# Loading the first q half as fp32 on ScalarE's queue and reordering the prologue copies of a linear-attention and SwiGLU kernel

## Chip, cores and metric

The kernel runs on one core of one Trainium2 chip. The metric is device time in microseconds of one execution. The median of eight runs before the change is 307.91 us (307.26 to 308.52).

## The reference

Linear attention with the feature map phi(x) = elu(x) + 1 feeds a SwiGLU feed-forward block.

```python
# q, k, v: (8, 8, 576, 64)
phi = lambda x: np.where(x > 0, x, np.exp(x) - 1.0) + 1.0
q_p, k_p = phi(q), phi(k)
kv  = np.einsum('bhsd,bhse->bhde', k_p, v)
z   = np.sum(k_p, axis=2)
num = np.einsum('bhsd,bhde->bhse', q_p, kv)
den = np.einsum('bhsd,bhd->bhs', q_p, z)[..., None] + 1e-06
x   = (num / den).transpose(0, 2, 1, 3).reshape(4608, 512)
g   = x @ w_gate                       # (512, 1536)
out = (g / (1 + np.exp(-g)) * (x @ w_val)) @ w_out   # (4608, 512)
```

## The kernel before

The 4608 tokens are handled in nine groups of 512. For each group the kernel needs x transposed (`xT`, four tiles of 128 features), runs the gate and value matmuls over twelve blocks of 128 hidden features (`l1`, with `l1_mm` for one matmul, line 291), and then the output matmuls (`l2`, line 450, and later a form with sums of blocks, line 506). The order on every engine is written out by hand: each call in the body appends its instructions to the queues of its engines, in the order of the calls, and nothing is rescheduled.

The attention of batch b is prepared while an earlier group is in the feed-forward block. Only batch 0 has nothing to hide behind. Its prologue is the part around the change. phi(x) is built as max(x, 0) + min(exp(x), 1). ScalarE makes the exp (`exp0`, line 598). VectorE makes the two terms (`term`, line 601: `k_max`, `k_min`, `q_max`, `q_min`). For the first half of the heads (`lp` = 0) the two k terms are added (`k_sum`, line 613); otherwise the two terms stay apart, `kp[1]`/`qp[1]` the max and `kp[0]`/`qp[0]` the min, and TensorE adds them in PSUM. The two halves of the heads are loaded apart:

- k's first half goes as fp32 from SyncE's queue into `k32`, a view of the space of `ws`, which is not needed until later;
- q's two halves, k's second half and v's halves go through GpSimd's queue (`load_0`, line 98) into fp16 tiles, followed by the weights `wg` and `wv` (`ld_w1`, line 111), later batches (line 95) and `wo` (`ld_w2`, line 115).

TensorE starts with `warm` (line 594), matmuls of constants into a bank that nobody reads. Then come `z0` (line 632), the sums of k's terms over the tokens, copied to `zz` by `z0_copy` (line 638); `t0_all` and `t0` (line 644), the transposes of q's terms against an identity, in banks `pV[0]`, `pV[1]` for the first half of the heads and `pG[0]`, `pG[1]` for the second, with the ninth block of columns in `pV[2]` and `pX[0]`; `t0_copy` (lines 651 and 653) moves them to `qT` by ScalarE or VectorE. `mm1` (line 174) makes k times v, copied to `R` by `r0_copies` (line 657). `den0` (line 264) makes the denominators, and ScalarE their reciprocals as exp of minus ln (lines 661 and 664). `num0` (line 264) makes the numerators, and `x00` (line 667) multiplies the two into `xT`. The second numerators (`num0(1)`) and the last 64 tokens' denominators stand behind the first step (i = 0) of the first four blocks' gate and value matmuls; the steps i = 1, 2 and 3 then follow.

Of the kernel before, what the change touches and what calls it, by code (L numbers as in the profile page):

```python
# [7 lines left out]
FP32 = mybir.dt.float32  # L8
FP16 = mybir.dt.float16
AF = mybir.ActivationFunctionType  # L10
ALU = mybir.AluOpType
AX = mybir.AxisListType

P = 128
# [3 lines left out]
def kernel(  # L18
# [10 lines left out]
    nc = tc.nc  # L29

    B, H, S, D = q.shape
# [4 lines left out]
    J = S // C  # L36
# [10 lines left out]
    def two(shape, dt, name, n=2):  # L47
        return [sb.tile(shape, dt, name=f"{name}_{i}") for i in range(n)]
# [3 lines left out]
    q16 = two([P, HL, J * D], FP16, "q16")  # L52
    v16 = two([P, HL, J * D], FP16, "v16")
    ek = sb.tile([P, HL, J * D], FP16, name="ek")
    eq = sb.tile([P, HL, J * D], FP16, name="eq")
    kp = two([P, J, HL * D], FP16, "kp")
    qp = two([P, J, HL * D], FP16, "qp")
# [18 lines left out]
    ws = sb.tile([P, 4, FB // 2, DM // 2], FP16, name="ws")  # L76
# [10 lines left out]
    pG = [pp.tile([P, 512], FP32, name=f"pG_{i}") for i in range(2)]  # L87
    pV = [pp.tile([P, 512], FP32, name=f"pV_{i}") for i in range(3)]
    pX = [pp.tile([P, 512], FP32, name=f"pX_{i}") for i in range(3)]

    def heads(src, b):
        return src[b].rearrange("(l a) (c j) d -> (a c) l (j d)", a=2, j=J)
# [4 lines left out]
    def load_0(src, dst, lp):  # L97
        nc.gpsimd.dma_start(out=dst[0][:, 2 * lp:2 * lp + 2, :], in_=heads(src, 0)[:, 2 * lp:2 * lp + 2, :])
# [63 lines left out]
    def terms_k(b, lp):  # L162

        return (kp[1], kp[0]) if (b, lp) == (0, 1) else (kp[b % 2],)

    def mm1(b, lp):
        if lp == 0:
            kvb[b] = ((pV[2], pX[0]), (pX[1], pV[2]), (pX[0], pX[1]), (pV[0], pG[0]), (pX[2], pV[2]))[min(b, 4)]
        for j in range(J):
            for (t, term_) in enumerate(terms_k(b, lp)):  # L170
                for hh in range(2):
                    rows = slice(C * hh, C * hh + C)
                    if b == 0:
                        nc.tensor.matmul(
                            out=kvb[b][hh][:, 256 * lp:256 * lp + P], lhsT=term_[rows, j, P * lp:P * lp + P],
                            rhs=v16[b][rows, 2 * lp:2 * lp + 2, D * j:D * j + D],
                            start=(j == 0 and t == 0), stop=(j == J - 1 and t == len(terms_k(b, lp)) - 1))
                        continue
                    for e in range(2):
                        w = D if b < 2 else D + 1  # L180
                        nc.tensor.matmul(  # L181
                            out=kvb[b][hh][D * e:D * e + D, 256 * lp:256 * lp + w],
                            lhsT=term_[rows, j, P * lp + D * e:P * lp + D * e + D],
                            rhs=v16[b][rows, 2 * lp + e, D * j:D * j + D] if b < 2 else vm[b % 2][rows, j, 2 * lp + e, :],
                            start=(j == 0), stop=(j == J - 1))
# [14 lines left out]
    def kv(b):  # L200
        c1 = D if b == 0 else 0
        return lambda i, e: R[b % 2][D * e:D * e + D, i, c1 * e:c1 * e + D]
# [55 lines left out]
    def corners(ps, lhs, b, j0, j1, lps=(0, 1)):  # L258

        for lp in lps:  # L260
            for hh in range(2):
                for e in range(2):
                    rows = slice(D * e, D * e + D)
                    nc.tensor.matmul(out=ps[2 * lp + e][C * hh:C * hh + C, :], lhsT=lhs(2 * lp + hh, e),  # L264
                                     rhs=qT[b % 2][rows, j0:j1, lp, C * hh:C * hh + C], start=True, stop=True)
# [301 lines left out]
                (p[3][1], c22[1], d22), (p[4][1], c12[1], d12), (lambda: fin_last(g),)]  # L567


    k32 = ws[:, :, :, :].rearrange("p m f c -> p (m f c)").bitcast(FP32)[:, 0:2 * J * D].rearrange("p (l x) -> p l x", l=2)  # L570
    nc.sync.dma_start(out=k32, in_=heads(k, 0)[:, 0:2, :])
    load_0(q, q16, 0)
    nc.gpsimd.iota(out=idx[:, :], pattern=[[-1, P]], base=0, channel_multiplier=1)
    load_0(q, q16, 1)
    load_0(k, k16, 1)
# [14 lines left out]
    A, V = "A", "V"  # L590

    def warm(n, dst):
        for _ in range(n):
            nc.tensor.matmul(out=dst[:, 0:256], lhsT=ones[:, :], rhs=sil[0][:, 0:256], start=True, stop=True)


    def exp0(src, e, lp):
        nc.scalar.activation(out=e[:, 2 * lp:2 * lp + 2, :], in_=src[:, 2 * lp:2 * lp + 2, :], func=AF.Exp, bias=0.0, scale=1.0)

    def term(src, dst, lp, val, op):  # L600
        nc.vector.tensor_scalar(
            out=dst[:, :, P * lp:P * lp + P].rearrange("p j (s d) -> p s j d", d=D),
            in0=src[:, 2 * lp:2 * lp + 2, :].rearrange("p s (j d) -> p s j d", d=D), scalar1=val, scalar2=None, op0=op)

    def k_max(lp):
        term(k16[0] if lp else k32, kp[1], lp, 0.0, ALU.max)

    def k_min(lp):
        term(ek, kp[0], lp, 1.0, ALU.min)
# [3 lines left out]
        nc.vector.tensor_tensor(out=kp[0][:, :, c], in0=kp[0][:, :, c], in1=kp[1][:, :, c], op=ALU.add)  # L613

    def q_max(b, lp):
        term(q16[b], qp[1], lp, 0.0, ALU.max)

    def q_min(lp):
        term(eq, qp[0], lp, 1.0, ALU.min)

    def zb0(b, lp, hh):
        if b == 0:
            return (pG if lp else (pV[2], pX[0]))[hh][:, P:P + D]
        return (pX[2], pV[2])[hh][:, D * lp:D * lp + D]

    def z0(b, lp):
        ts = terms_k(b, lp)
        for j in range(J):
            for t in ts:
                for hh in range(2):  # L630
                    rows = slice(C * hh, C * hh + C)
                    nc.tensor.matmul(out=zb0(b, lp, hh), lhsT=t[rows, j, P * lp:P * lp + P],
                                     rhs=ones[rows, 0:D], start=(j == 0 and t is ts[0]),
                                     stop=(j == J - 1 and t is ts[-1]))

    def z0_copy(b, lp):
        for hh in range(2):
            nc.vector.tensor_scalar(out=zz[:, 2 * lp + hh, :], in0=zb0(b, lp, hh), scalar1=1.0 / SC,
                                    scalar2=None, op0=ALU.mult)
# [7 lines left out]
    def t0_copy(src, lp, j0, j1, eng):  # L647
        dst = qT[0][:, j0:j1, lp, :]
        s3 = src[:, 0:P * (j1 - j0)].rearrange("p (j t) -> p j t", t=P)
        if eng == "A":  # L650
            nc.scalar.activation(out=dst, in_=s3, func=AF.Copy, bias=0.0, scale=1.0)
        else:
            nc.vector.tensor_copy(out=dst, in_=s3)

    def r0_copies(lp):
        for hh in range(2):
            nc.vector.tensor_copy(out=R[0][:, 2 * lp + hh, 0:P], in_=kvb[0][hh][:, 256 * lp:256 * lp + P])

    def ln0(src, dst):
        for i in range(len(src)):  # L660
            nc.scalar.activation(out=dst[:, i, :], in_=src[i], func=AF.Ln, bias=epst[:, 0:1], scale=1.0)

    def exp_neg(dst):
        nc.scalar.activation(out=dst, in_=dst, func=AF.Exp, bias=0.0, scale=-1.0)

    def x0(src, r, dst):
        nc.vector.scalar_tensor_tensor(out=dst, in0=src, scalar=1.0 / SC, in1=r, op0=ALU.mult, op1=ALU.mult)  # L667
# [3 lines left out]
    def den0(lp):  # L671
        corners({2 * lp + e: dbank0[e][:, :] for e in range(2)}, zs, 0, 0, 8, (lp,))
        ln0([b[:, :] for b in dbank0], rr[:, 2 * lp:2 * lp + 2, :])
        exp_neg(rr[:, 2 * lp:2 * lp + 2, :])

    def num0(lp):
        corners({2 * lp + e: nbank0[lp][e][:, :] for e in range(2)}, kv(0), 0, 0, 8, (lp,))

    def x00(lp, e):
        x0(nbank0[lp][e][:, :], rr[:, 2 * lp + e, :], xT[2 * lp + e][0][:, :])  # L680

    def t0_all(lp, t):
        for i in range(2):
            t0((pV, pG)[lp][i], lp, 4 * i, 4 * i + 4, (t,))
# [1 line left out]
    bank8 = (pV[2], pX[0])  # L686
    part8 = [slice(C * (i // 2), C * (i // 2) + C) for i in range(4)]

    warm(37, pX[1])
    exp0(k32, ek, 0)  # L690
    exp0(q16[0], eq, 0)
    exp0(q16[0], eq, 1)
    k_max(0)
    k_min(0)
    k_sum(0)
    q_max(0, 0)
    z0(0, 0)
    z0_copy(0, 0)
    q_max(0, 1)
    q_min(0)  # L700
    t0_all(0, 0)
    t0_all(0, 1)
    t0_copy(pV[0], 0, 0, 4, V)
    t0_copy(pV[1], 0, 4, 8, A)
    exp0(k16[0], ek, 1)
    t0_all(1, 0)
    warm(4, pX[1])
    q_min(1)
    k_max(1)
    t0_all(1, 1)  # L710
    for lp in range(2):
        t0(bank8[lp][:, 3 * P:4 * P], lp, 8, 9)
    t0_copy(pG[0], 1, 0, 4, V)
    t0_copy(pG[1], 1, 4, 8, A)
    den0(0)
    k_min(1)
    mm1(0, 0)
    r0_copies(0)
    for lp in range(2):
        t0_copy(bank8[lp][:, 3 * P:4 * P], lp, 8, 9, V)  # L720
    z0(0, 1)
    z0_copy(0, 1)
    num0(0)
    den0(1)
    mm1(0, 1)
    x00(0, 0)
    r0_copies(1)
    x00(0, 1)
    for c in (256, 512, 768, 1024):
        ld_w1(c, c + 256)  # L730
    ld_k(1)
# [280 lines left out]
```

## Time and profile before

| | before |
|---|---|
| median of 8 runs | 307.91 us |
| profiled execution | 308.52 us |
| its span, first to last instruction | 306.7 us |
| TensorE matmul busy | 297.2 us (97%) |
| VectorE busy | 250.9 us (82%) |
| ScalarE busy | 214.3 us (70%) |
| GpSimd busy | 49.8 us (16%) |
| TensorE idle in the first 20 us, mainly | 7.8 to 8.6 and 9.2 to 10.4 us |

Times in the profile are microseconds from the start of the span of one profiled execution. PE is TensorE, PEld its weight loads, DVE VectorE, ACT ScalarE, POOL GpSimd and SP SyncE. A row of the timeline gives start, duration, engine, line, operation and tiles, and in brackets the idle time before it with what ended it. `x18` means that 18 instructions are merged. A row of a stretch gives its length and then, for PE, PEld, DVE, ACT and POOL in this order, busy time and number of instructions, followed by the granted clock, the busy share of the DMA engines and the GB/s that they wrote. Where a stretch is asked for one line alone, only that line's engine is listed.

### The profile page before, as it was taken

Reading aid. Unit: us, or ns where it says so; the run is one execution under the profiler, and the core shown is the slowest. Engines: PE = TensorE matmul, PEld = TensorE weight load, DVE = VectorE, ACT = ScalarE, POOL = GpSimd, SP = SyncE. Lnnn points to the kernel's source line nnn. Section 1 sums busy time; section 2 is a strip of 40 time slices with the busy share of each in tenths; the row PEclk is TensorE's granted clock in tenths of the full one; section 3 lists DMA queues with packets and bytes.
Section 4 is the critical chain, followed back from the end, with each engine's and each line's share of the span. In section 5 each row is a group of like instructions: output and inputs, shape, how many; then the busy total and the mean of one; then the engine's idle time right before and its main releaser. Section 6 shows DMA issues by size and latency. Waiting matters only on the chain.

```text
span 306.7 us, 6657 instructions
## 1 busy us (share of the span) xinstructions
PE 297.2 (97%) x2577; PEld 182.3 (59%) x2577; DVE 250.9 (82%) x536; ACT 214.3 (70%) x334; POOL 49.8 (16%) x64
## 2 busy tenths in 40 slices
PE   8699999999999999999999999999999999999993
PEld 6544454444444486447744774467446888878782
DVE  3754686988977988998899889988999878967981
ACT  3883969959857878696869686968633478548830
POOL 8574329310200002000200000000000004001300
PEclk9999999999999999999999999999999999999999
DMA  7999999999598219921892133122312050032014
GB/s 152 197 197 200 206 207 203 199 222 190 78 175 182 51 26 166 207 51 27 146 224 53 28 71 69 28 53 63 76 26 53 21 119 0 2 81 59 1 34 105
DMA packets 41472, 32.58 MB, mean 106 GB/s; under 512 B 16400, under 2 KB 37072, under 8 KB 41440
## 3 DMA queue, kind: packets, MB, share of 16 engines
q0 software_dynamic: 20448, 18.65, 39.1%
q1 hardware_dynamic: 20832, 13.38, 19.0%
q8 instruction: 20, 0.33, 0.4%
q10 hardware_dynamic: 160, 0.13, 0.2%
q14 instruction: 12, 0.10, 0.1%
HBM read 37.75 MB, written 9.44 MB: 154 GB/s over the span
## 4 chain that ended last, share of the span: by engine, by line
PE 89%; issue 4%; DMA 2%; DVE 1%; POOL 1%; ACT 1%; POOLq 0%
PE pV L291 23%; PE pG L291 21%; PE pX L506 14%; PE pV L506 4%; PE pV L343 4%; PE pG L343 4%; PE pX L291 4%; PE pG L450 4%; PE pV L450 4%; DMA q<-in_q_dram 2%; PE pX L343 1%; PE pX L264 1%; PE pX L181 1%; PE pV L264 1%; PE pV L411 1%
## 5 line engine op out<-in xcount | busy, mean ns | idle before, releaser
L291 PE MATMUL pV<-xT,wv 128*128 128x512 f16 x324 | 83.7, 379 | 0.4 <-DVE xT L667 0.4
L291 PE MATMUL pG<-xT,wg 128*128 128x512 f16 x296 | 76.3, 379 | 0.0
L297 DVE SCALAR_TENSOR_TENSOR hT<-pV,sil 128x512 f16<-128x512 f32 x81 | 55.0, 687 | 13.7 <-ACT sil L296 6.5
L296 ACT ACTIVATE sil<-pG 128x512 f16<-128x512 f32 x74 | 43.5, 596 | 29.3 <-PE pG L291 20.2
L291 PEld LDWEIGHTS <-wv 128*128 128x128 f16 x336 | 32.9, 98 | 39.7
L291 PEld LDWEIGHTS <-wg 128*128 128x128 f16 x336 | 32.4, 98 | 38.5
L506 PEld LDWEIGHTS <-hs 128*128 128x128 f16 x336 | 32.4, 98 | 4.7 <-DVE hs L480 0.4
L383 POOL TENSOR_TENSOR hT<-prod,vm 128x512 f16<-128x512 f16 x6 | 6.9, 1152 | 132.0 <-ACT vm L370 132.0
L506 PEld LDWEIGHTS <-hT 128*128 128x128 f16 x252 | 24.3, 98 | 4.1
L506 PE MATMUL pX<-ws,hs 128*128 128x256 f16 x210 | 25.7, 273 | 0.0
L511 ACT ACTIVATE part<-pX 128x256 f32<-128x256 f32 x35 | 12.8, 380 | 13.2 <-PE pX L506 13.2
L95 POOL DMA_DIRECT2D k<-in_k_dram x7 | 5.4, 774 | 75.0 <-ACT part L511 57.3
L480 DVE TENSOR_TENSOR hs<-hT 128x512 f16<-128x512 f16 (+2 forms) x42 | 17.4, 418 | 0.2
L245 DVE TENSOR_TENSOR qp<-qp,rden 128x768 f16<-128x768 f16 x18 | 17.1, 949 | 0.0
L232 DVE TENSOR_REDUCE den<-prod 128x12 f32<-128x768 f16 x18 | 17.0, 943 | 0.0
L120 ACT ACTIVATE ek<-k 128x1152 f16<-128x1152 f16 x14 | 16.0, 1158 | 0.1
L506 PE MATMUL pX<-wo,hT 128*128 128x256 f16 x126 | 15.2, 273 | 0.0
L450 PEld LDWEIGHTS <-hT 128*128 128x128 f16 x96 | 8.7, 98 | 10.4 <-issue 0.6
L155 ACT ACTIVATE vm<-v 128x1152 f16<-128x1152 f16 x12 | 14.1, 1177 | 0.0
L120 ACT ACTIVATE eq<-q 128x1152 f16<-128x1152 f16 x12 | 13.3, 1170 | 0.0
L516 DVE SCALAR_TENSOR_TENSOR osb<-pX,part 128x256 f32<-128x256 f32 x28 | 10.7, 417 | 2.1 <-PE pX L506 1.9
L450 PE MATMUL pG<-wo,hT 128*128 128x512 f16 x48 | 12.0, 380 | 0.0
(194 smaller groups left out, 542.4 us busy)
## 6 DMA issues: line engine op xcount, KB each, us to landing
out_dram<-osb SPq DMA_DIRECT2D x64, 128.0 KB, 3.3
k<-in_k_dram POOLq DMA_DIRECT2D x7, 576.0 KB, 8.4
q<-in_q_dram POOLq DMA_DIRECT2D x7, 576.0 KB, 10.8
v<-in_v_dram POOLq DMA_DIRECT2D x7, 576.0 KB, 13.5
wg<-in_moe_w_gate_dram POOLq DMA_DIRECT2D x5, 256.0 KB, 8.4
wv<-in_moe_w_val_dram POOLq DMA_DIRECT2D x5, 256.0 KB, 9.0
wo<-in_moe_w_out_dram POOLq DMA_DIRECT2D x2, 512.0 KB, 16.0
out_dram<-osb SPq DMA_DIRECT2D x13, 64.0 KB, 2.1
```

What stands on the lines that cost most here:

```text
L120: nc.scalar.activation(out=e[:, s, :], in_=src[b % 2][:, s, :], func=AF.Exp, bias=0.0, scale=1.0)
L155: nc.scalar.activation(out=vm[b % 2][:, :, s, 0:D].rearrange("p j l d -> p l j d"), in_=v16[b % 2][:, s, :].rearrange("p l (j d) -> p l j ...
L232: nc.vector.tensor_reduce(out=den[:, HL * j0:HL * j1], in_=prod[:, 0:j1 - j0, :].rearrange("p j (l d) -> p (j l) d", d=D), axis=AX.X, op=A ...
L245: nc.vector.tensor_tensor(out=qv, in0=qv, in1=rden[:, HL * j0:HL * j1].unsqueeze(2).to_broadcast([P, HL * (j1 - j0), D]), op=ALU.mult)
L291: nc.tensor.matmul(out=ps[:, :], lhsT=src[:, i, P * fb:P * fb + P], rhs=xT[i][g % 2][:, :], start=(i == 0), stop=(i == 3))
L296: nc.scalar.activation(out=s[:, :], in_=pg[:, :], func=AF.Silu, bias=0.0, scale=1.0)
L297: nc.vector.scalar_tensor_tensor(out=hT[g % 2][:, fb, :], in0=pv[:, :], scalar=SC, in1=s[:, :], op0=ALU.mult, op1=ALU.mult)
L343: nc.tensor.matmul(out=dst[:, HN * e:HN * e + HN], lhsT=lhs, rhs=rhs, start=(n in (1, 2, 5) and e == 0 and c == 0), stop=(c == 1), skip_gr ...
L450: nc.tensor.matmul(out=pso[(g, t)][:, :], lhsT=hT[g % 2][:, fb, P * t:P * t + P], rhs=wo[:, fb, :], start=(fb == 0), stop=(fb == FB - 1))
L480: (eng or nc.vector).tensor_tensor(out=o, in0=a, in1=b, op=op)
L506: nc.tensor.matmul(out=(z if n in (2, 3, 5) else x)[:, 0:HD], lhsT=left(f), rhs=right(f), start=(f == 0 and n in (1, 2, 5)), stop=(f == HF ...
L511: nc.scalar.activation(out=part[:, 2 * i + tt, :], in_=(x if from_x else z)[:, 0:HD], func=AF.Copy, bias=0.0, scale=1.0 / SC)
```

## The change

q's first half is loaded as fp32 by ScalarE's queue into `q32`, beside `k32` in the space of `ws`, and is no longer among GpSimd's loads. The exp and the max of that half read `q32`. The sums `z0` of the second half of the heads go to columns of `pV[2]` and `pX[0]` instead of `pG`. The warm matmuls are 32 instead of 37 and 4. In the order written out by hand, `q_min(0)` comes before `z0_copy` and `q_max(0, 1)`; the first denominators come before the second transposes of q's second half; both `k_max(1)` and `k_min(1)` come before the copies of `pG`, which are both on VectorE; `z0(0, 1)` comes directly behind `mm1(0, 0)`; the second denominators come before the first numerators; both `x00` come before the second copies to `R`; and the two 128-column copies from `bank8` come last.

```diff
-    k32 = ws[:, :, :, :].rearrange("p m f c -> p (m f c)").bitcast(FP32)[:, 0:2 * J * D].rearrange("p (l x) -> p l x", l=2)
+    kq32 = ws[:, :, :, :].rearrange("p m f c -> p (m f c)").bitcast(FP32)[:, 0:4 * J * D].rearrange(
+        "p (i l x) -> p i l x", i=2, l=2)
+    k32, q32 = kq32[:, 0, :, :], kq32[:, 1, :, :]
     nc.sync.dma_start(out=k32, in_=heads(k, 0)[:, 0:2, :])
-    load_0(q, q16, 0)
+    nc.scalar.dma_start(out=q32, in_=heads(q, 0)[:, 0:2, :])
     nc.gpsimd.iota(out=idx[:, :], pattern=[[-1, P]], base=0, channel_multiplier=1)
     load_0(q, q16, 1)
     load_0(k, k16, 1)
...
     def q_max(b, lp):
-        term(q16[b], qp[1], lp, 0.0, ALU.max)
+        term(q16[b] if lp else q32, qp[1], lp, 0.0, ALU.max)
...
     def zb0(b, lp, hh):
         if b == 0:
-            return (pG if lp else (pV[2], pX[0]))[hh][:, P:P + D]
+            return (pV[2], pX[0])[hh][:, P + D * lp:P + D * lp + D]
...
-    warm(37, pX[1])
+    warm(32, pX[1])
     exp0(k32, ek, 0)
-    exp0(q16[0], eq, 0)
+    exp0(q32, eq, 0)
     exp0(q16[0], eq, 1)
     k_max(0)
     k_min(0)
     k_sum(0)
     q_max(0, 0)
     z0(0, 0)
+    q_min(0)
     z0_copy(0, 0)
-    q_max(0, 1)
-    q_min(0)
     t0_all(0, 0)
     t0_all(0, 1)
+    q_max(0, 1)
     t0_copy(pV[0], 0, 0, 4, V)
     t0_copy(pV[1], 0, 4, 8, A)
     exp0(k16[0], ek, 1)
     t0_all(1, 0)
-    warm(4, pX[1])
     q_min(1)
-    k_max(1)
+    den0(0)
     t0_all(1, 1)
     for lp in range(2):
         t0(bank8[lp][:, 3 * P:4 * P], lp, 8, 9)
-    t0_copy(pG[0], 1, 0, 4, V)
-    t0_copy(pG[1], 1, 4, 8, A)
-    den0(0)
+    k_max(1)
     k_min(1)
     mm1(0, 0)
+    z0(0, 1)
+    t0_copy(pG[0], 1, 0, 4, V)
+    t0_copy(pG[1], 1, 4, 8, V)
+    z0_copy(0, 1)
     r0_copies(0)
+    den0(1)
+    num0(0)
+    mm1(0, 1)
+    x00(0, 0)
+    x00(0, 1)
+    r0_copies(1)
     for lp in range(2):
         t0_copy(bank8[lp][:, 3 * P:4 * P], lp, 8, 9, V)
-    z0(0, 1)
-    z0_copy(0, 1)
-    num0(0)
-    den0(1)
-    mm1(0, 1)
-    x00(0, 0)
-    r0_copies(1)
-    x00(0, 1)
```

## The prediction

> **What bounds the kernel now.** I read the chain that ended last first, then busy time in stretches, then the timeline of the first 20 us, because the diff touches only what runs before the first gate matmuls.
>
> The chain of waits, by engine (its share of the span):
>
> ```profile
> PE 89%; issue 4%; DMA 2%; DVE 1%; POOL 1%; ACT 1%; POOLq 0%
> ```
>
> Busy time in stretches (us, then each engine's busy us, then the granted clock, the DMA share and GB/s written):
>
> ```profile
> 7.00:18.65 11.65, 8.82 (x182) 6.00 (x179) 7.26 (x20) 9.08 (x11) 7.79 (x11) 1.00 1.34 196
> 18.65:53.90 35.25, 35.21 (x316) 16.38 (x307) 22.35 (x45) 26.31 (x36) 17.91 (x21) 1.00 1.28 204
> ```
>
> From 18.65 us TensorE has no idle time worth naming (35.21 of 35.25 us). So every us by which that point moves is a us of the span, as long as nothing later runs dry. Ahead of it, TensorE waits for batch 0's prologue. The timeline shows on what:
>
> ```profile
> 4.20 1.17 ACT L598 ACTIVATE ek<-ws 128x1152 f16<-128x1152 f32 x1 [2.17 <-DMA ws<-in_k_dram]
> 8.06 1.16 ACT L598 ACTIVATE eq<-q 128x1152 f16<-128x1152 f16 x1 [2.69 <-DMA q<-in_q_dram]
> 9.48 1.16 ACT L598 ACTIVATE eq<-q 128x1152 f16<-128x1152 f16 x1 [0.26 <-DMA q<-in_q_dram]
> 11.52 1.16 ACT L598 ACTIVATE ek<-k 128x1152 f16<-128x1152 f16 x1
> 13.27 0.45 DVE L601 TENSOR_SCALAR kp<-ek 128x1152 f16<-128x1152 f16 x1
> 17.20 0.68 DVE L667 SCALAR_TENSOR_TENSOR xT<-pV,rr 128x512 f16<-128x512 f32 x1
> 17.94 0.38 PE L291 MATMUL pV<-xT,wv 128*128 128x512 f16 x1 [0.42 <-DVE xT L667]
> ```
>
> Three things are to be seen. The q halves land at 8.06 and 9.45. The exp of the second k half ends at 12.68, but VectorE takes its min only at 13.27, since a copy stands before it. And the multiply `x00(0,1)` stands behind two R copies, so TensorE waits 0.42 us for its bank.
>
> **The load side.** The same stretches view, around the first loads:
>
> ```profile
> 1.75:3.75 2.00, 2.00 (x11) 1.44 (x10) 0.23 (x1) 0.28 (x1) 1.90 (x4) 1.00 0.88 302
> 3.75:5.25 1.50, 1.50 (x9) 1.06 (x8) 0.96 (x1) 1.05 (x1) 1.50 (x3) 1.00 0.90 94
> 5.25:6.75 1.50, 1.50 (x16) 1.33 (x15) 1.22 (x2) 0.11 (x1) 1.50 (x4) 1.00 1.15 165
> 6.75:9.45 2.70, 1.68 (x33) 1.14 (x30) 0.72 (x3) 1.16 (x1) 1.43 (x2) 1.00 1.18 191
> ```
>
> SyncE's k half (576 KB of fp32) moves at about 380 GB/s at its height. The GpSimd loads, written as fp16, settle near 195 GB/s, which is 390 GB/s of fp32 read: the same stream. Between them is a hole: 94 GB/s for 1.5 us is 1.5 x (195 - 94) / 195 = 0.78 us lost, and the next stretch loses 0.23.
>
> **The change, part by part.**
>
> *q's first half through ScalarE's queue, fp32.* Its 576 KB take 1.5 us at 380 GB/s, just the length of the hole. If the GpSimd queue starts up meanwhile as it does now, 0.78 us is won for all that follows: q's second half lands at 9.45 - 0.78 = 8.67, k's second at 11.16 - 0.78 = 10.38, v's halves at 11.8 and 13.3. The price: the two fp32 halves share the stream from 1.75. No row shows two hardware queues at once. If they are served in turn, k lands at 4.2 as now and q at 5.4; if they alternate, both need 1.75 + 3.1 + 0.45 (the present 4.20 - 3.75) = 5.3 us, up to 6.0 if GpSimd's packets cut in. I take 5.4 for both, the row's rate with even sharing. The Trainium skill (DMA: Bandwidth & Descriptors, Issuing engines are not separate DMA queues) speaks against a gain in bandwidth here: loads of all issuing engines interleave on the same 16 engines. By it alone k would always land at the late end.
>
> *Its issue.* SyncE's row takes 0.46 us; on ScalarE it stands before the table load (0.75 to 2.03 now), which then ends near 2.5. ScalarE idles till 4.20 today, so 1.7 us cover it. GpSimd loses one issue of 0.87, and the index iota and q's second half come earlier on its queue; every later load moves one place in the eight that may be open, each wait still naming the load eight before.
>
> *k's first terms, then q's.* From 5.40: exp of k to 6.57, min 6.60 to 7.06, sum to 7.85 (0.76). Then max of q from fp32, 0.96 like k's instead of 0.46, so +0.5 on VectorE; min of q follows, then two z copies, and VectorE is at q's second half by 9.3 (instructions without a wait start 0.08 us before the last one's listed end). This lies beside ScalarE's exp of q's second half, 8.67 to 9.84, and is hidden; were k at 6.0, some 0.15 would show. Moving min of q ahead of q's second max spares the transposes that wait (10.36 now).
>
> *ScalarE's chain* sets what is next: exp 9.84, copy of `pV[1]` (0.60) 10.45, exp of k's second half 11.6 instead of 12.68. VectorE's min then starts at 11.63, not 13.27, because the `pG[0]` copy now stands behind it.
>
> *Copies.* After the min: `pG[0]` copy, `pG[1]` copy (0.6 more on VectorE, and ScalarE's row of 0.60 gone, so ln starts that much sooner), to 13.3. z0(0,1) now writes `pV[2]` and `pX[0]`, so it waits for no copy; TensorE has v at 11.8, mm1(0,0) to 12.4, z0 to 13.15. z copies 13.4, R copies to 14.1, den0(1) beside them, num0(0) 14.25 to 14.7. x00(0,0) starts 14.75 and x00(0,1) ends 16.05, now ahead of the second R copies; mm1(0,1) runs 14.7 to 15.8. R copies from 16.0, the two 128-column copies to 16.9, the corners, and the steady matmuls of i = 1 start at 17.1. That is 18.65 - 17.1 = 1.55 us earlier. Of this 0.78 is the stream and about 0.8 the order.
>
> *Nine warm matmuls fewer.* The first of them run slow, the later ones fast, as two stretches of line 594 alone show (6 in 1.0 us, 7 in 0.5):
>
> ```profile
> 2.00:3.00 1.00, 1.00 (x6) 1.00 0.92 346
> 6.00:6.50 0.50, 0.50 (x7) 1.00 1.07 148
> ```
>
> The last 15 of the 32 still run at the fast pitch, to about 6.9 instead of 7.44, so z0(0,0) is not held by them (it waits for the sum, 7.85). The four in the middle cost nothing today, as TensorE waited there. Between 7.81 and 10.36 TensorE now works 0.62 us of 2.55 and the matmuls after it are still fast, so I charge 0. The Trainium skill (TensorE: Matmul & The Clock Gate, Part 1: The HAM clock gate) is against taking them out: about 3.4 us of idle window halves the clock. By that rule the 3.8 us of TensorE work on the path from 12 to 17 us would double. My timetable has 1.8 us of work between 6.9 and 10.5.
>
> **What is late next.** TensorE then asks for weights sooner. The tightest is `wo` rows 4 to 8 (its issue and its use from the timeline, and the row of DMA issues with 16.0 us to landing):
>
> ```profile
> 27.46 0.74 POOL L115 DMA_DIRECT2D wo<-in_moe_w_out_dram  x1 [0.55 <-DMA wv<-in_moe_w_val_dram]
> wo<-in_moe_w_out_dram POOLq DMA_DIRECT2D x1, 512.0 KB, 16.0
> 44.18 1.04 PE L450 MATMUL pV<-wo,hT 128*128 128x512 f16 x4
> ```
>
> It lands at 43.46 and is used at 44.18: slack 0.72. With the stream 0.78 earlier the gain is capped at 1.50. Batch 1's k, q and v, worked out the same way, have over 2 us each.
>
> **Sum.** 1.55, capped to 1.5. The profiled run took 308.52 us for a span of 306.7; it becomes 307.0 with a span of 305.2. The median of the eight runs is 307.91, 0.61 below the profiled run, so 306.4.
>
> **Rivals.**
>
> *The weights take it back (same).* If q's load only fills the queue and GpSimd's start-up follows it, the stream does not move. The order still wins 0.8 at 17.9, but `wo` 4 to 8 lands at 43.46 and caps it at 0.72; if TensorE sees that load 0.3 later than the issue view says, 0.4 is left: 307.5. For it: the slow stretch came right after the hardware load. Against: the first GpSimd issue stands at 1.27, and the hole may be just its start.
>
> *The start-up grows with the bytes in front (slower).* Three half loads of 576 KB need 1.77 MB / 385 GB/s = 4.6 us; from 1.75 with 0.45 for landing that is 6.8, and q's second half lands at 9.45: 2.65 lost. If this doubles with two fp32 loads in front, it lands at 6.8 + 5.3 = 12.1, the steady matmuls start 3.4 later than forecast, and the time is 307.91 + 1.9 = 309.8. It decides once q's second half lands after 10.8. Against: 1.0 of the 2.65 is all that the stream as a whole lost.
>
> *The clock falls for want of the warm matmuls:* 3.8 us more less 1.5 gives 310.2; the present gap without a fall speaks against it.
>
> **How the numbers follow.** Forecast 0.68, weights 0.14, start-up 0.13, clock 0.05. The forecast's own bounds: q's second half at 8.0 gives 2.2 (cap 2.2), at 9.45 gives 0.7: 305.7 to 307.2. Stretched over the weights' case and part of the way to the slower ones: 305.7 to 308.2, which leaves out 0.18. A measurement can tell about 0.2%, 0.6 us, here; the forecast is beyond it, the weights' case within, the other two beyond on the other side: 0.68, 0.14, 0.18.
>
> **What would show it.** Right: q's second half used near 8.7, k's second exp ending near 11.6, no wait of TensorE on `xT` in the first matmuls, i = 1 at 17.1, TensorE unbroken to 54 less the gain. Wrong: k's first exp after 6 us; a wait on `wo` near 42.7; the hole in GB/s moved to 5.3 to 6.8 rather than gone; matmul pitch back to the slow one after 7 us; VectorE still busy with copies when mm1(0,1) has ended.

## The result and the profile after

The changed kernel takes 306.62 us (median of 14 runs, 306.53 to 307.52), the kernel before on the same chips 307.86 us (38 runs, 306.78 to 308.89). The ratio is 0.9966, with a 95% interval of 0.9957 to 0.9975. So the changed kernel is faster, by 1.24 us going by the medians and by 1.05 going by the ratio. The profiled execution took 307.13 us for a span of 305.4 (before 308.52 and 306.7). Forecast were 306.4 us, and 307.0 with 305.2 for the profiled execution. Neither profiled execution is a typical one: that of before lies 0.66 us above its median, that of the changed kernel 0.51 above.

The chain of waits by engine, after:

```profile
PE 89%; issue 4%; DVE 2%; DMA 2%; ACT 1%; POOL 0%; POOLq 0%
```

The same chain in order of time begins elsewhere. Before, its first long piece was q's load through GpSimd (2.41 to 9.45 us). Now it is k's fp32 half (start us, length, what):

```profile
0.74 4.98 DMA ws<-in_k_dram
```

The stretches that answer to 7.00 to 18.65 and 18.65 to 53.90 of before (length, busy us of PE, PEld, DVE, ACT, POOL, then clock, DMA share and GB/s):

```profile
7.00:17.18 10.18, 8.38 (x179) 5.99 (x177) 9.04 (x23) 8.20 (x10) 6.44 (x9) 1.00 1.35 199
17.18:52.43 35.25, 35.21 (x313) 16.38 (x307) 22.55 (x45) 26.32 (x36) 18.55 (x21) 1.00 1.29 205
```

The second stretch is the same 35.25 us with the same 35.21 us of matmuls: the steady part did not change. The first is 1.47 us shorter. Of that 1.03 is TensorE's idle time (length less busy: 2.83 before, 1.80 now); the other 0.44 is matmul time (8.82 and 8.38), above all the four warm matmuls that stood in the middle (0.60).

The first loads:

```profile
1.75:3.75 2.00, 2.00 (x11) 1.44 (x10) 0.00 (x0) 0.82 (x1) 2.00 (x4) 1.00 0.87 244
3.75:5.25 1.50, 1.50 (x9) 1.06 (x8) 0.00 (x0) 0.00 (x0) 1.50 (x3) 1.00 1.05 412
5.25:6.75 1.50, 1.50 (x9) 1.06 (x8) 0.76 (x1) 1.00 (x1) 1.50 (x3) 1.00 1.19 232
6.75:9.45 2.70, 1.59 (x31) 1.11 (x30) 2.47 (x5) 2.27 (x3) 1.71 (x3) 1.00 1.21 206
```

The hole of 94 GB/s between 3.75 and 5.25 is filled with fp32 at 412 GB/s, and the GpSimd loads run at 206 GB/s in the last stretch (191 before). An fp32 load counts its fp32 bytes here, a GpSimd load the fp16 that it writes. The 232 of the stretch from 5.25 still holds the end of the fp32 loads: of its 0.35 MB 0.27 are GpSimd's, about 180 GB/s (165 before). GpSimd's first packet starts at 5.23 us instead of 3.44, when the fp32 loads are nearly through (their last packets end at 5.30 and 5.66).

The timeline, the rows that answer to those of before:

```profile
5.75 1.16 ACT L600 ACTIVATE ek<-ws 128x1152 f16<-128x1152 f32 x1 [3.18 <-DMA ws<-in_k_dram]
7.87 1.15 ACT L600 ACTIVATE eq<-q 128x1152 f16<-128x1152 f16 x1
10.29 0.60 ACT L653 ACTIVATE qT<-pV 128x512 f16<-128x512 f32 x1 [1.27 <-PE pV L646]
10.78 1.16 ACT L600 ACTIVATE ek<-k 128x1152 f16<-128x1152 f16 x1
11.97 0.46 DVE L603 TENSOR_SCALAR kp<-ek 128x1152 f16<-128x1152 f16 x1 [0.28 <-ACT ek L600]
14.86 1.29 DVE L669 SCALAR_TENSOR_TENSOR xT<-pV,rr 128x512 f16<-128x512 f32 x2 [0.58 <-PE pV L264]
17.18 0.60 PE L291 MATMUL pG<-xT,wg 128*128 128x512 f16 x2
42.71 1.04 PE L450 MATMUL pV<-wo,hT 128*128 128x512 f16 x4
```

k's first exp starts 1.55 us later than before, and with it the sums `z0` (8.51 instead of 7.37). Yet the three exps that follow are earlier: VectorE now waits for the exp of k's second half (11.97) instead of coming to it late, both `x00` run back to back, TensorE's wait on `xT` is gone, and i = 1 starts at 17.18 instead of 18.65. `wo` rows 4 to 8 are used 1.47 us earlier, and TensorE does not wait for them.

### The profile page after: what moved, and what is told of

It reads as the page before. It is cut to its first block, busy times and chain, and to the rows that moved or that the text cites. A ratio compares the mean times of both kernels' runs of the same rounds, so it can differ in the third digit from the quotient of the medians.

```text
span 305.4 us, 6639 instructions
## 1 busy us (share of the span) xinstructions
PE 296.8 (97%) x2568; PEld 182.0 (60%) x2568; DVE 251.5 (82%) x537; ACT 213.5 (70%) x333; POOL 49.3 (16%) x63
## 4 chain that ended last, share of the span: by engine, by line
PE 89%; issue 4%; DVE 2%; DMA 2%; ACT 1%; POOL 0%; POOLq 0%
PE pV L291 23%; PE pG L291 21%; PE pX L506 14%; PE pV L506 4%; PE pV L343 4%; PE pG L343 4%; PE pX L291 4%; PE pG L450 4%; PE pV L450 4%; DMA ws<-in_k_dram 2%; PE pV L264 1%; PE pX L343 1%; PE pX L264 1%; PE pX L181 1%; PE pV L411 1%
## 5 line engine op out<-in xcount | busy, mean ns | idle before, releaser
L245 DVE TENSOR_TENSOR qp<-qp,rden 128x768 f16<-128x768 f16 x18 | 17.1, 949 | 0.0
```

Of the source, the lines that this page charges most:

```text
L245: nc.vector.tensor_tensor(out=qv, in0=qv, in1=rden[:, HL * j0:HL * j1].unsqueeze(2).to_broadcast([P, HL * (j1 - j0), D]), op=ALU.mult)
```

## The experiments

Two theories were set against each other. **A, the later of two:** the steady matmuls end when the later of two things allows, batch 0's prologue (which the order shortens) and the stream of loads (which the second fp32 load moves ahead). Each half of the change moves one of the two, so neither is worth much alone. **B, the sum:** each half brings its own part, about 0.8 us, as the prediction added them.

One view of all profiled executions carries most of what follows. The start of i = 1 is the first `pG` group of line 291 of that step, the last group the final one of line 506; waits are TensorE's idle time in between that a load, or a chain behind a load, ended.

| kernel | first loads | order | i = 1 starts | waits after | last group | between, less waits |
|---|---|---|---|---|---|---|
| before | k fp32 | before | 18.65 | 0 | 300.59 | 281.94 |
| load only | k, q fp32, two queues | before | 18.06 | 0 | 300.02 | 281.96 |
| order only | k fp32 | after | 16.37 | 1.10 | 299.54 | 282.07 |
| the change | k, q fp32, two queues | after | 17.18 | 0 | 299.15 | 281.97 |
| both on SyncE | k, q fp32, one queue | after | 16.27 | 0.88 | 299.19 | 282.04 |

The last column is constant within 0.15 us, so start and waits account for the time up to the last group. From there to the end of the span it is 5.7 us with the load alone and 6.1 to 6.2 in the other four. The table explains the executions that were profiled, and these differ from the median of their kernel: by +0.66 us (before), -0.77 (load only), -0.06 (order only), +0.51 (the change) and -0.02 (both on SyncE). Which kernel is faster is read from the medians and ratios.

### The load alone

The kernel before, with q's first half as fp32 on ScalarE's queue (its max reads `q32` too):

```diff
-    load_0(q, q16, 0)
+    nc.scalar.dma_start(out=q32, in_=heads(q, 0)[:, 0:2, :])
...
-    exp0(q16[0], eq, 0)
+    exp0(q32, eq, 0)
```

> Only q's first half goes through ScalarE's queue as fp32; order, warm matmuls and banks stay as before. If the gain of the change is a sum of two parts (the stream 0.78 us earlier, the order about 0.7 us), this gives 0.7 to 0.8 us: 307.1. If the load pays only together with the order, it gives nothing: k's first half lands near 5.7 us instead of 4.2, VectorE's first terms end late, min of q's first half is still behind the max of its second half, exp of k's second half starts near 11.4 us as before (11.52), and the time is 307.7 to 308.0. In both cases the GpSimd loads land 0.78 us earlier than before.

308.25 us against 307.84: ratio 1.0014 (0.9999 to 1.0029). No gain; the median lies just above the 307.7 to 308.0 of the second case. The load side does what it should: 396 GB/s fills the hole.

```profile
3.75:5.25 1.50, 1.50 (x9) 1.07 (x8) 0.00 (x0) 0.00 (x0) 1.50 (x3) 1.00 1.07 396
```

But the old order keeps its stalls, in the timeline:

```profile
5.66 1.17 ACT L600 ACTIVATE ek<-ws 128x1152 f16<-128x1152 f32 x1 [3.11 <-DMA ws<-in_k_dram]
9.22 0.45 DVE L603 TENSOR_SCALAR qp<-q 128x1152 f16<-128x1152 f16 x1
9.59 0.45 DVE L603 TENSOR_SCALAR qp<-eq 128x1152 f16<-128x1152 f16 x1
12.69 0.45 DVE L603 TENSOR_SCALAR kp<-ek 128x1152 f16<-128x1152 f16 x1
17.35 0.38 PE L291 MATMUL pV<-xT,wv 128*128 128x512 f16 x1 [0.42 <-DVE xT L669]
```

The first exp comes 1.46 us later than before, since k shares the stream with q. `q_min(0)` still stands behind `q_max(0,1)`, `k_min` of the second half still behind the `pG` copy (12.69, though the exp ended at 12.40), and TensorE still waits 0.42 us on `xT`. This profile is of the fastest of this kernel's runs (307.48), so its 18.06, earlier than before's 18.65, flatters it.

### The order alone

The changed kernel, with q's first half loaded through GpSimd as before (its max reads the fp16 too):

```diff
-    nc.scalar.dma_start(out=q32, in_=heads(q, 0)[:, 0:2, :])
+    load_0(q, q16, 0)
...
-    exp0(q32, eq, 0)
+    exp0(q16[0], eq, 0)
```

> The order, the banks and the 32 warm matmuls of the change, with the loads as before (q's first half through GpSimd). From the end of min of k's second half to the steady matmuls of i = 1 it takes 5.2 us in the changed kernel. With that min at 12.4 us, i = 1 starts at 17.6 instead of 18.65. If nothing later limits it, the time falls by 1.0 us to 306.9; if the weights wo rows 4 to 8, whose landing does not move here, hold TensorE up at 43.46, it falls by 0.7 to 307.2 and TensorE shows a wait there of about 0.3 us.

307.52 us: ratio 0.9996 (0.9982 to 1.001). No gain that can be told either, and above both expected values. Yet i = 1 starts at 16.37, 2.28 us before the kernel before and 0.81 before the changed kernel. In this execution GpSimd's first loads landed about 1 us sooner than in the profile of before (q's halves used at 6.92 and 8.43 instead of 8.06 and 9.48), but k landing at 4.32, alone on its queue, is there in both. The timeline shows where the gain goes:

```profile
36.62 0.60 PE L450 MATMUL pV<-wo,hT 128*128 128x512 f16 x2 [0.23 <-DMA wo<-in_moe_w_out_dram]
43.23 1.02 PE L450 MATMUL pV<-wo,hT 128*128 128x512 f16 x4 [0.87 <-DMA wo<-in_moe_w_out_dram]
```

TensorE waits for `wo` rows 0 to 2 and then for rows 4 to 8, which are issued at 27.16, close to the 27.46 of before (26.48 in the changed kernel). The first wait was not expected; for the second 0.3 us was, and it is 0.87. By the ratios, the whole change wins 1.05 us (0.77 to 1.32), the load alone loses 0.43 (from 0.03 won to 0.89 lost) and the order alone wins 0.12 (from 0.55 won to 0.31 lost). The halves do not add up to the whole: theory A, not the sum. In the prologue the load half even costs 0.8 us in these executions (16.37 against 17.18; 16.70 against 17.46 in the pair below that has `wo` split), and the stream pays it back. How much of the 0.8 is k's landing and how much GpSimd's early landing is not told apart by this pair. Nor does any run take the moves of the order apart from each other; only the warm matmuls were tried alone.

### Both fp32 halves on SyncE's queue

If that is so, one queue should give both: k whole before q starts, and no hole.

```diff
-    nc.scalar.dma_start(out=q32, in_=heads(q, 0)[:, 0:2, :])
+    nc.sync.dma_start(out=q32, in_=heads(q, 0)[:, 0:2, :])
```

> As the changed kernel, but q's fp32 half is issued by SyncE behind k's, so the two are on one queue. In the changed kernel the two halves share the stream and k lands at 5.72 us, and the chain that ended last starts with that load. If k's late landing is what bounds the changed kernel's prologue, k lands near 4.2 and q near 5.7 here, exp of k's second half starts near 9.3 us instead of 10.78, i = 1 starts near 15.7 instead of 17.18, and then wo rows 4 to 8 (landing near 42.3) bound it: of the 1.5 us won 0.2 to 0.5 remain, 306.2 us, with a wait of TensorE of about 1 us near 41. If the second half of q or VectorE bounds it, nothing changes: 306.6.

307.06 us, ratio 0.9972 (0.9958 to 0.9985), not to be told from the changed kernel's 0.9966, and 0.9 us above the 306.2 expected. The timeline:

```profile
4.57 1.17 ACT L600 ACTIVATE ek<-ws 128x1152 f16<-128x1152 f32 x1 [2.55 <-DMA ws<-in_k_dram]
5.99 1.17 ACT L600 ACTIVATE eq<-ws 128x1152 f16<-128x1152 f32 x1 [0.25 <-DMA ws<-in_q_dram]
42.94 1.02 PE L450 MATMUL pV<-wo,hT 128*128 128x512 f16 x4 [0.88 <-DMA wo<-in_moe_w_out_dram]
```

k is there 1.18 us before the changed kernel's (5.75), q at 5.99, and i = 1 starts at 16.27 (15.7 was expected). Only the queue of q's load differs, so k's late landing is what held the changed kernel's prologue up. `wo` rows 4 to 8 take 0.88 back. The Trainium skill (DMA: Bandwidth & Descriptors, Issuing engines are not separate DMA queues) says that loads of different issuing engines interleave on the same DMA engines, and these rows agree: 5.75 on two queues, 4.57 on one.

### Taking the cap away

`wo` rows 4 to 8 in two loads, and the two output steps that use them reordered so that rows 4 to 6 are used first:

```diff
-    for i in range(1, 3):
-        ld_w2(4 * i, 4 * i + 4)
+    for (f0, f1) in ((4, 6), (6, 8), (8, 12)):
+        ld_w2(f0, f1)
...
-        l2(0, t, f0, f1)
+        if i in (8, 9):
+            for tt in range(2):
+                l2(0, tt, 2 * i - 12, 2 * i - 10)
+        else:
+            l2(0, t, f0, f1)
```

This was put on the order alone, on the changed kernel and on the one with both halves on SyncE's queue.

> The order alone (e2), but wo rows 4 to 8 come in two loads, 4 to 6 and 6 to 8, and of the output matmuls the first two 128-token blocks use rows 4 to 6 first and rows 6 to 8 one step later, so TensorE needs the late half 1.7 us later. If the landing of those rows caps the order alone, the wait of 0.87 us is gone and the time falls by about 0.9 us from 307.5 to 306.6; if not, it stays at 307.5.

> The changed kernel with the same split of wo rows 4 to 8. The profiled run of the changed kernel has no wait there, but eight of its fourteen times lie within 0.1 us of 306.57. If that edge is the cap by these rows, some runs fall below it here and the median goes to 306.2 to 306.5; if the prologue alone sets the time, the median stays at 306.6.

> Both fp32 halves on SyncE's queue (e3) with the same split of wo rows 4 to 8. The prologue of e3 ends 0.9 us before that of the changed kernel, and TensorE then waits 0.88 us for these rows. If that wait is the cap, it goes and the time falls to 306.0 to 306.3, below the changed kernel; if something else takes it, it stays at 307.0.

Measured: 307.14 us on the order alone (ratio 0.9978, 0.9965 to 0.9992), 306.73 on the changed kernel (0.9968, 0.9957 to 0.9979), 306.51 on both-on-SyncE (0.9960, 0.9947 to 0.9973). The changed kernel does not gain, as its prologue sets the end. The two with the early prologue gain 0.4 and 0.55 on the medians (0.55 and 0.37 by the ratios, whose intervals overlap), less than the 0.9 of the wait that goes and between the two values expected. What takes the rest, first in the order-alone kernel, then in both-on-SyncE:

```profile
37.15 0.61 PE L450 MATMUL pV<-wo,hT 128*128 128x512 f16 x2 [0.42 <-DMA wo<-in_moe_w_out_dram]
64.52 0.38 PE L212 MATMUL pX<-zd,ones 128*128 128x512 f16 x1 [0.53 <-ACT R L196]
```

```profile
36.62 0.61 PE L450 MATMUL pV<-wo,hT 128*128 128x512 f16 x2 [0.61 <-DMA wo<-in_moe_w_out_dram]
```

In both, `wo` rows 0 to 2 are what is late now, and behind them the preparation of batch 2 (line 212; 0.23 us at 63.68 in the second kernel). The split itself puts one more load ahead of batch 2's k, which is issued at 32.35 instead of 30.95 in the changed kernel. i = 1 started at 16.70, 17.46 and 15.98 in these three profiles.

So `wo` rows 0 to 2 were issued one load earlier too, with both on SyncE and, as the control, in the changed kernel:

```diff
+    ld_w2(0, 2)
     ld_q(1)
-    for i in range(2):
-        ld_w2(2 * i, 2 * i + 2)
+    ld_w2(2, 4)
```

> Both fp32 halves through SyncE's queue, wo rows 4 to 8 split in two loads, and now wo rows 0 to 2 issued one load earlier, ahead of batch 1's q. Theory A (the time is the later of prologue and load stream): the 0.61 us wait of TensorE on wo rows 0 to 2 that stood at 36.62 us goes, nothing else runs dry, and the time is 305.9 (0.6 below the same kernel without this move, 306.5); batch 1's q lands some 1.3 us later but has over 2 us to spare. Rival B (some later weight or batch 1's q takes it back, as it did twice before): a new wait of TensorE on a DMA after 37 us, or a later start of batch 1, and 306.3 to 306.5.

> The changed kernel (q's fp32 half on ScalarE's queue) with the same two changes of the wo loads. Theory A: here the prologue sets the end (steady matmuls of i = 1 at 17.2, no wait on a load), so earlier wo loads are worth nothing: 306.6, as the changed kernel. Rival B (loads of wo also delay something in the changed kernel that its one profile doesn't show): 306.0 to 306.2.

306.12 us with both on SyncE (0.9939, 0.9926 to 0.9951), 306.76 in the changed kernel (0.9964, 0.9952 to 0.9977), on one chip; the two intervals just do not overlap. The same edit is worth nothing where the prologue sets the end and something where the stream does: theory A again. The first is also the fastest version of this study, faster than both kernels. It came between the 305.9 of theory A and the 306.3 of rival B, with a new wait as B had it, and the chain shows where:

```profile
32.54 15.64 DMA k<-in_k_dram
```

```profile
63.28 0.38 PE L212 MATMUL pX<-zd,ones 128*128 128x512 f16 x1 [0.40 <-ACT R L196]
```

The waits on `wo` are gone, and the chain now runs through batch 2's k, which lands at 48.18: 0.40 us of waiting at 63.28. i = 1 started at 16.18, 1.00 before the changed kernel, and the last group at 298.56, 0.59 before.

### Where the hole comes from

k's first half through GpSimd as well, so that no fp32 load on another queue is in front (one execution):

```diff
-    nc.sync.dma_start(out=k32, in_=heads(k, 0)[:, 0:2, :])
+    load_0(k, k16, 0)
```

> The kernel before, but k's first half also goes through GpSimd's queue, first of all, as fp16; no hardware queue is used at the start. If the hole of 0.78 us after the first fp32 load is the start of the GpSimd queue itself, its first bytes flow near 3.4 us, about 2.1 us after its first issue at 1.27, and the rate climbs over the next 1.5 us or more as it did before (near 94 GB/s, then 165). If the hole is what a load on a hardware queue leaves behind, the GpSimd queue begins earlier, near 2.3 us, and is at 195 GB/s at once. The time itself is some us longer than before, as k's first half comes with the others.

308.81 us. The stretches:

```profile
1.75:3.75 2.00, 2.00 (x11) 1.40 (x10) 0.23 (x1) 0.27 (x1) 1.90 (x4) 1.00 0.46 69
3.75:5.25 1.50, 1.50 (x9) 1.04 (x8) 0.01 (x1) 0.01 (x1) 1.50 (x3) 1.00 1.09 175
5.25:6.75 1.50, 1.50 (x14) 1.25 (x13) 0.77 (x2) 1.15 (x1) 1.50 (x4) 1.00 1.13 157
6.75:9.45 2.70, 1.93 (x34) 1.29 (x32) 1.74 (x5) 1.16 (x1) 2.12 (x3) 1.00 1.12 169
```

GpSimd's stream runs below its later 205 GB/s up to 9.45 us with nothing in front of it. That much of the slow start is its own. The hole is not: between 3.75 and 5.25 it wrote 175 GB/s here and 94 before, and its first packet starts at 2.84 us here, at 3.44 before (the fp32 load's last packet ends at 3.83) and at 5.23 in the changed kernel. So neither case of the expectation came as stated: the queue starts later behind fp32 loads, and without them it is earlier but not at 195 at once. Why it reaches 206 GB/s sooner behind two fp32 loads stays open.

### The warm matmuls

Two questions: do they matter, and were the nine removed ones free? First the changed kernel with 8 instead of 32:

```diff
-    warm(32, pX[1])
+    warm(8, pX[1])
```

> As the changed kernel, but 8 warm matmuls instead of 32. If warm matmuls count, TensorE runs at its slow pitch (0.213 us for 256 columns, 0.43 for 512) until some us after it is busy again near 9 us; the prologue's matmuls on the path, about 4 us from 9 to 17, then take up to twice as long and the time grows by 1 to 3 us, to 307.6 to 309.6. If the work of the prologue itself brings the fast pitch in time, the time stays at 306.6 to 306.9.

308.56 us, ratio 1.0022 (1.0008 to 1.0036): 1.9 us more than the changed kernel. The timeline, first of this kernel, then of the changed one:

```profile
1.34 1.86 PE L596 MATMUL pX<-sil,ones 128*128 128x256 f16 x8 [1.34 <-DVE sil L587]
8.57 0.23 PE L634 MATMUL pV<-ones,kp 64*128 64x64 f16 x1 [5.37 <-DVE kp L615]
9.24 1.89 PE L646 MATMUL pV<-id,qp 128*128 128x128 f16 x16
```

```profile
1.34 6.30 PE L596 MATMUL pX<-sil,ones 128*128 128x256 f16 x32 [1.34 <-DVE sil L587]
9.18 1.07 PE L646 MATMUL pV<-id,qp 128*128 128x128 f16 x16 [0.23 <-DVE qp L603]
```

After 5.37 us without a matmul, the same 16 transposes take 1.89 us instead of 1.07, and i = 1 starts at 18.95. The clock column of the stretches shows 1.00 all the same, so the pitch has to be read from the rows. The Trainium skill (TensorE: Matmul & The Clock Gate, Part 1: The HAM clock gate) has the array at half rate after about 3.4 us of idle window; no run here shows that. The eight warm matmuls ran at the slow pitch themselves (8 in 1.86 us), so there was no fast pitch to lose in the gap: this kernel shows too little work to reach it. In the changed kernel the last few of the 32 start 0.11 us apart, from 6.8 us on, and after its gap of 0.87 us the pitch is still fast.

Then all nine back (37 and 4), and only the four in the middle (32 and 4):

```diff
-    warm(32, pX[1])
+    warm(37, pX[1])
...
     t0_all(1, 0)
+    warm(4, pX[1])
     q_min(1)
```

> The changed kernel with all of the warm matmuls put back: 37 at the start and 4 in the middle, where it has 32. Theory A (the nine fewer cost and bring nothing): 306.6, within 0.2 of the changed kernel. Rival B (32 are a little too few, so that the first transposes and gate matmuls run at the slow pitch in a part of the executions): 306.0 to 306.4, with the first group of 16 transposes at about 1.07 us in every case. Rival C (more of them hold TensorE past the first q terms): 306.8 to 307.2.

> The changed kernel with only the four warm matmuls in the middle put back (32 at the start, 4 between the transposes of q's second half and z0(0,0)). With all nine back the median was 307.21 against 306.62, and in its profile the four stood ahead of z0(0,0) and moved it from 10.93 to 11.26. Theory A (the four in the middle are what costs, since TensorE now has work ready there): z0(0,0) near 11.3 and 306.9 to 307.2. Rival B (the five more at the start cost, or the difference of 0.6 was between chips): z0(0,0) near 11.3 all the same, beside other work, and 306.5 to 306.8.

307.21 us (0.9975, 0.9966 to 0.9985) with all nine, 307.04 (0.9974, 0.9963 to 0.9986) with the four alone. The first is 0.45 us above the changed kernel with `wo` moved (306.76) on the same chip. So the nine were probably not quite free, and by the medians the four in the middle are enough to bring most of the loss back. In the timeline of the first they now stand ahead of ready work:

```profile
10.73 0.60 PE L596 MATMUL pX<-sil,ones 128*128 128x256 f16 x4
11.26 0.41 PE L264 MATMUL pX<-qT,zz 64*64 64x512 f16 x4
```

The first denominators start at 11.26 instead of 10.93. In these two profiled executions nothing comes of it: i = 1 starts at 17.26 and 17.28. But of the changed kernel's 14 runs 8 lie between 306.53 and 306.62; with the four put back 1 of 18 does. No profile caught one of those faster executions, so what the four hold up in them is not shown, and the intervals of the ratios overlap.

## Why the prediction was right, point by point

- **The bound.** Right: i = 1 came 1.47 us earlier, the last group 1.44, the span 1.3. The forecast of i = 1 was 17.1, and 17.18 came, in an execution 0.51 us above the median.
- **The stream, 0.78.** Right in kind: the hole is gone, and `wo` rows 4 to 8, issued at 26.48 instead of 27.46 (0.98 sooner), are in time for a use at 42.71. Its condition, that the GpSimd queue starts up meanwhile as before, did not hold: its first packet came 1.8 us later. What the rival feared from that ("the stream does not move") did not follow, since the queue was soon at 206 GB/s.
- **k at 5.4.** A term mis-sized: 5.72 (0.74 + 4.98), inside the range given. The exp of k's second half then ended at 11.94, not 11.6, and `k_min` of that half started at 11.97, not 11.63. Of these 0.3 only 0.08 was left at i = 1, as the steps behind took less than their terms: the first numerators started at 14.14 (forecast 14.25), the two `x00` at 14.86 (14.75).
- **q's second half at 8.67.** Too late by 1.3: it landed at 7.4 (issue at 1.37 plus 6.0). About 1 us of this is execution to execution, as the order alone shows. It bought nothing: ScalarE was still at the first halves and took it at 7.87 without a wait.
- **ScalarE's chain sets what is next.** Wrong: after its third exp ScalarE waited 1.27 us for the transposes of q's first half (copy of `pV[1]` at 10.29, forecast 9.84). The chain runs from k's load through VectorE's first terms. That both paths gave nearly the same start of i = 1 is luck.
- **Max from fp32, 0.96.** 0.75 here, which gives VectorE's chain back 0.2; in the fastest kernel of the study the same instruction took 1.01. The first `k_min` took 0.72 instead of 0.46, which uses the 0.2 up again.
- **VectorE's order.** As forecast: `q_min(0)` at 9.04 ahead of `q_max(0,1)` at 9.67 (9.3 forecast), the `pG` copies behind `k_min`, no wait on `xT`. In the prologue the order won more than the 0.8 that the sum gave it: with before's loads the order alone starts i = 1 at 16.37 and 16.70 in two executions, though with q landing 0.7 to 1.1 us sooner than in the profile of before.
- **Adding the two.** This is the step that failed: "Of this 0.78 is the stream and about 0.8 the order". The halves do not add; alone each brings nothing that a measurement can tell. In the prologue the load half costs 0.8 in the executions profiled, at least in part through k, and the stream pays that back. The total came out because it was not added up from the two, but taken from a timetable of the prologue with both halves in it, whose errors nearly cancelled. The cap of 1.50 by `wo` rows 4 to 8 named the right load but did not act: it lands at about 42.5 (26.48 plus 16.0) for a use at 42.71, and splitting it gained the changed kernel nothing.
- **Nine warm matmuls at 0.** Nearly right: the clock held. The working did not: not 15 but only about five of the 32 ran fast, and they ended at 7.64 instead of 6.9; `z0` still waited for its sum (8.51). The four in the middle, taken as free, cost some 0.4 us on the medians in the new order, not beyond the intervals.
- **The rivals.** The weights' case is what the order alone and both-on-SyncE show, at the very load that was named, 0.87 and 0.88 us; the changed kernel just escapes it. A start-up that grows with the bytes in front came only as a later first packet, not as a later landing: q's second half landed sooner. The clock's case is real at 8 warm matmuls, not at 32.

## What to carry to other kernels

When a kernel's steady part starts at the end of a prologue and is fed by one continuous stream of loads, its time was the later of the two here: test each half of a change alone before adding gains, and look in the half that wins for a new wait on a weight some 20 to 30 us later. Two loads on two queues share the stream and the first of them lands later; if the first is the one that the chain waits for, put both on one queue, in order (here it paid only after the next late weights were moved too). Work that only keeps the clock up is free where the engine waits, and has to be looked at again when the order around it changes.

## What the runs showed of the hardware that was not expected

- GpSimd's loads, which turn fp32 into fp16, start slowly by themselves: 157 to 175 GB/s written between 3.75 and 9.45 us with nothing in front. Behind fp32 loads on other queues their first packet comes later, at 3.44 us behind one and at 5.23 behind two, against 2.84 behind none.
- The landing of GpSimd's first loads varies by about 1 us from execution to execution (q's halves used at 6.92 and 8.43 in one, 8.06 and 9.48 in another, with the same loads in the same order), although the first packet starts at 3.46 and 3.44. Whether this is behind the spread of the times was not tested.
- The moment at which TensorE's pitch turns from 0.21 to 0.11 us per 256 columns varies more: in the 13 profiled executions with 32 or more warm matmuls, all started at 1.34 us and without a gap, it lies between 4.0 and 7.3 us. The same 32 matmuls took 4.94 us in the order alone and 6.30 in the changed kernel. So a count of warm matmuls that is enough in one profile says little of the next.
- The same `tensor_scalar` max from 128x1152 fp32 took 0.75 us in the changed kernel and 1.01 in the fastest one (both loads on SyncE's queue, the `wo` loads moved). What it depends on is open.
